# Loads of weights in an attention kernel: each quarter behind the latest transpose of probabilities, instead of four in a row

## Chip, cores and metric

The kernel runs on one core of one Trainium2 chip. The metric is the device time of one execution in microseconds; the time before is the median of three runs. Engines are named TensorE (PE in the profile, its weight loads PEld), VectorE (DVE), ScalarE (ACT), GpSimd (POOL) and SyncE (SP, which here only issues transfers).

## What is computed

Block-causal attention, then a dense mixture of four experts, then a feed-forward layer with a softmax and a layer norm in its middle:

```python
def reference(...):
    # attention: q, k, v are (4, 8, 576, 64); a query sees its block of 64 and all blocks before
    scores = scale * np.matmul(q, k.transpose(0, 1, 3, 2))
    scores = np.where(mask, scores, -1000000000.0)
    attn = np.exp(scores - np.max(scores, axis=-1, keepdims=True))
    attn = attn / (np.sum(attn, axis=-1, keepdims=True) + 1e-09)
    x = heads_to_columns(np.matmul(attn, v))          # (2304, 512)
    # mixture: w1 (4, 512, 1024), w2 (4, 1024, 512)
    for e in range(4):
        out += p[:, e:e + 1] * (np.maximum(x @ w1[e], 0.0) @ w2[e])
    # second layer: h = out @ w_in, softmax gate, layer norm, ln @ w_out
```

## The kernel before

The 2304 tokens are 18 tiles of 128 rows (`TILES`, L38): two tiles hold the first 64 rows of two batches each, called (0,0) and (2,0), and the others are tile i = 1 to 4 of batch b, called (b,i) here. They are worked through in that order. A tile (b,i) has four pairs of heads, and attention goes in steps of one pair (for i = 4, one head): TensorE makes the scores `sps`, VectorE their maximum `nm`, ScalarE the exponentials `p` (L959) and their f16 high part `hl` (L963), VectorE the low part (L964). SyncE then issues one transposing transfer per pair, `pT<-hl` (L974, in `step_b`), and TensorE multiplies pT with v into `pv` (L993). A pT of a tile with i = 1, 2, 3, 4 shows in the order as 6, 10, 14, 18 x 128. When a tile's four pairs are done, it is scaled, split in two f16 parts `xh` and transposed to `xT`, the mixture's input.

Every f32 operand of the mixture is kept as two f16 parts, so each product is three. A weight (w1 or w2 of one expert, 2 MB) goes through `w_steps` (L174): `load` takes the only buffer `stage`; four calls of `load_part` (L189) load a quarter of 512 KB each; four of `square` (L207, ScalarE) and one `scale` give the factor; four of `split` (L221) write the high part on ScalarE (L232) and the low part on VectorE (L235).

The mixture is cut in phases by expert. A phase consists of units from `phase_units` (L478): units of the first layer (`hps`, L372), whose result is evicted by ScalarE and VectorE to `hch`, and of the second (`ops`, L394). Phase 0 covers tiles 0 to 5 with expert 0, phases 1 to 3 the same tiles with the other experts, phases 4 to 7 the other twelve tiles. Phase 4 takes the weights of phase 3 once more; phase 5 loads those of expert 0 again.

The order of the work is set in two places. The loop at L1345 decides what the program emits next: an attention step, or the next entry of the list `moe` (a unit, or a piece of a weight's preparation that `spread` (L1305) has put between units). After each step it also runs up to three tasks of the list `bg`, which holds the rest of w2 of expert 0, then w1 of expert 1, then the loads and squares of w2 of expert 1:

```python
            for _ in range(3):
                if bg and bg[-1][0] <= at1.n:
                    bg.pop()[1]()
```

A scheduler then places each instruction on its engine's queue by its dependencies and by the program's order, and may put a load far ahead of the instructions that were written before it. `after` (L142) adds a dependency that costs no semaphore: it only keeps one instruction behind another in such an order. Each queue runs in order, so a transfer on SyncE's queue that waits, or is long in issue, holds up those behind it. The object `InOrder` (L81), through which all of SyncE's transfers go, is why they all show line L91.

Of the kernel before, what the change touches and what calls it, by code (L numbers as in the profile page):

```python
# [60 lines left out]
def tile_kernel(  # L61
# [17 lines left out]
    strict = [False]  # L79
# [62 lines left out]
    def after(ins, other):  # L142

        tc.add_manual_dep(
            ins.ins, other.ins.name, mybir.DependencyInfo(mybir.DependencyClass.NoSync, mybir.DependencyReason.DATA),
            reason="pace",
        )
# [11 lines left out]
    marks = {}  # L159
# [14 lines left out]
    def w_steps(key, src, bits, inv, tag, load_eng, rows=None, hi_eng=None, place_raw="stage", known=False, less=False):  # L174

        single = key in ("w_in", "w_out")
        n = F if key == "w_in" else D if key == "w_out" else src.shape[1]
        k = 4096 // n
        q = k // 4
# [9 lines left out]
        def load_part(c):  # L189
            def f():  # L190
                if single:
                    load_eng.dma_start(out=stage[key][:, c * 1024:(c + 1) * 1024], in_=src[:, c * 1024:(c + 1) * 1024])
                    return
                sv = stage[key].rearrange("p (k f) -> p k f", k=k)
                dv = src.rearrange("(k p) f -> p k f", p=128)
                m = n // 2 if less and c < 2 else n
                load_eng.dma_start(out=sv[:, c * q:(c + 1) * q, :m], in_=dv[:, c * q:(c + 1) * q, :m])
            return f

        def scale_rows(c):  # L200
# [152 lines left out]
    def flush():  # L353

        while pend:
            pend.pop(0)()
        while tail:
            tail.pop(0)()
# [382 lines left out]
    class Attention:  # L741
# [192 lines left out]
        def step_b(self, n):  # L934
            t, p, heads, last = self.steps[n]
            b, i = TILES[t]
            ps, nm = self.sPS.pop(n), self.nm_.pop(n)
            if t not in self.sums:
                self.sums[t] = sp.tile([128, NH], F32, tag="sums", name="sums")
            sums = self.sums[t]  # L940
            L = 64 + 128 * i
            W = 512 if i == 0 else 2 * L
            key = (t, p)
            if key not in self.hl_:
                self.hl_[key] = self.hlp.tile([128, 2304], F16, tag="hl", name="hl")
            hl = self.hl_[key]
            parts = [heads] if i == 0 else [(h,) for h in heads]
            for j, hh in enumerate(parts):
                pf = self.pp.tile([128, 576], F32, tag="p32", name="p32")
                n_ = W if i == 0 else L  # L950
                c0 = 0 if i == 0 else (hh[0] % 2) * L
                for x, h in enumerate(hh):
                    if i == 0:
                        src, dst = ps[:, 0, x * 128:(x + 1) * 128], pf[:, x * 128:(x + 1) * 128]
                    elif i < 4:
                        src, dst = ps[:, j, 0:L], pf[:, 0:L]
                    else:
                        src, dst = ps[:, :, 0:288], pf[:, 0:L].rearrange("p (a c) -> p a c", a=2)
                    act.activation(  # L959
                        out=dst, in_=src, func=AF.Exp, bias=nm[:, j + x:j + x + 1], scale=SCALE,  # L960
                        accum_out=sums[:, h:h + 1],
                    )
                anc["A"] = act.activation(out=hl[:, c0:c0 + n_], in_=pf[:, 0:n_], func=AF.Copy)  # L963
                anc["D"] = vec.tensor_tensor(  # L964
                    out=hl[:, W + c0:W + c0 + n_], in0=pf[:, 0:n_], in1=hl[:, c0:c0 + n_], op=ALU.subtract
                )
            if not last:
                return
            del self.hl_[key]
            if 3 <= t < FREE and n % 3 == 0:  # L970
                tt = xps[1].tile([128, 18, 128], F16, tag="xT3", name="pT")
            else:
                tt = self.tp.tile([128, 18, 128], F16, tag="pT", name="pT")
            x = sync.dma_start_transpose(out=tt[:, 0:2 * W // 128, :], in_=hl[:, 0:2 * W])  # L974
            if n < 2:
                marks["sync"] = x
            self.pT_[key] = tt

        def step_c(self, n):
# [235 lines left out]
    def load_near(odd):  # L1215
        at1.raws["near"] = near
        c = 0 if odd else S - NEAR
        src = kT[:, 0].rearrange("d (p x) s -> d p x s", x=2)[:, :, odd, c:c + NEAR]
        sync.dma_start(out=near.rearrange("d (p x) s -> d p x s", x=2)[:, :, odd], in_=src)

    def load_v(v, a, b):
        sync.dma_start(out=v, in_=vC[0, :, a:b])
        for j in range(a, b):
            at1.raws["v", 0, j] = [v[:, j - a]]
# [5 lines left out]
    def norm():  # L1230
# [9 lines left out]
        n=[lambda: load_near(0), lambda: load_near(1)], v=[lambda: load_v(vrs[0], 0, 3), lambda: load_v(vrs[1], 3, 5)], p=[load_p],  # L1240
# [64 lines left out]
    def spread(units, *spans):  # L1305

        todo = []
        for a, b, tasks in spans:
            todo += [(a + (b - a) * (k + 1) / len(tasks), fn) for k, fn in enumerate(tasks)]
        todo.sort(key=lambda x: x[0])  # L1310
        res = []
        for j, u in enumerate(units):
            while todo and todo[0][0] <= j:
                res.append((None, todo.pop(0)[1], 0.0))
            res.append(u)
        return res + [(None, fn, 0.0) for _, fn in todo]
# [9 lines left out]
    bg = [(2, fn) for fn in p1 + q1]  # L1326
    bg += [(14, fn) for fn in p2 + q2] + [(32, fn) for fn in p3]
    moe = phase_units(0, [(t, 1) for t in range(6)], psh)
    post = q3
    for j in range(1, 5):  # L1330
        us = phase_units(j, GROUPS[j // E], psh)
        n = len(us)
        if j == E - 1:
            moe += spread(us, (0, 0.1 * n, post))
            post = []
            continue
        pa, qa = next_w()
        pb, qb = next_w()
        moe += spread(us, (0, 0.1 * n, post), (0.1 * n, 0.5 * n, pa + qa), (0.5 * n, 0.9 * n, pb))
        post = qb  # L1340
    moe.reverse()
    bg.reverse()
    tpe = tdv = 0.0
    n1 = len(p2 + q2 + p3)
    while at1.more:  # L1345
        t, u, cost = moe[-1] if moe else (-1, None, 0)
        ok = t is None or t in ready and len(bg) <= n1
        if not ok or tdv <= tpe + 2.0:
            flush()
            at1.step()  # L1350
            a, c = at1.cost()
            tdv, tpe = tdv + (a * 1.2 if at1.n < SLOW else PACE + c), tpe + c
            for _ in range(3):
                if bg and bg[-1][0] <= at1.n:
                    bg.pop()[1]()
        else:
            moe.pop()
            u()
            if cost:
                flush()  # L1360
            tpe += cost
# [11 lines left out]
    n = len(moe)  # L1373
# [12 lines left out]
    for j in (5, 6, 7):  # L1386
        tasks = [[], [], [], []]
        pa, qa = next_w()
        pb, qb = next_w()
# [16 lines left out]
        post = qb  # L1406
# [174 lines left out]
```

## Time and profile before

| | |
|---|---|
| median of three runs | 1113.18 us (1112.07 to 1114.56) |
| the profiled execution | 1114.37 us, its span 1112.6 us |
| mean granted TensorE clock | 0.989 |
| busy: TensorE | 1048.0 us (94%) |
| busy: VectorE | 797.7 us (72%) |
| busy: ScalarE | 514.1 us (46%) |
| busy: GpSimd | 182.1 us (16%) |
| pT transfers | 68, median 4.3 us from issue to landing |
| loads into `stage` of 512 KB | 50, median 6.0 us from issue to landing |

Attention, with phases 0 to 3 and part of phase 4 between its steps, lies in the first 515 us or so; the rest is mixture and second layer. Shares over the whole span are averages over these parts. [...]

### The profile page before, as it was taken

Reading aid. Unit: us, or ns where it says so; the run is one execution under the profiler, and the core shown is the slowest. Engines: PE = TensorE matmul, PEld = TensorE weight load, DVE = VectorE, ACT = ScalarE, POOL = GpSimd, SP = SyncE. Lnnn points to the kernel's source line nnn. Section 1 sums busy time; section 2 is a strip of 40 time slices with the busy share of each in tenths; the row PEclk is TensorE's granted clock in tenths of the full one; section 3 lists DMA queues with packets and bytes.
Section 4 is the critical chain, followed back from the end, with each engine's and each line's share of the span. In section 5 each row is a group of like instructions: output and inputs, shape, how many; then the busy total and the mean of one; then the engine's idle time right before and its main releaser. Section 6 shows DMA issues by size and latency. Waiting matters only on the chain.

```text
span 1112.6 us, 20532 instructions
## 1 busy us (share of the span) xinstructions
PE 1048.0 (94%) x8064; PEld 657.2 (59%) x8064; DVE 797.7 (72%) x1758; ACT 514.1 (46%) x1107; POOL 182.1 (16%) x176
## 2 busy tenths in 40 slices
PE   4579889799999999999999999999999999999998
PEld 4456666465555556555576767666667674444443
DVE  7898788738768677436677656674879558999883
ACT  5667676646755455433443424232446453333222
POOL 4874633422115421000000000000000000000000
PEclk9999989799999999999999999999999999999999
DMA  9868987928877857332531212330344311434333
GB/s 303 247 164 159 249 184 163 222 79 192 193 120 178 177 147 157 64 61 48 174 114 58 77 39 76 115 133 29 95 138 128 107 27 29 95 86 88 74 85 85
DMA packets 225600, 137.95 MB, mean 124 GB/s; under 512 B 184544, under 2 KB 192736, under 8 KB 225504
## 3 DMA queue, kind: packets, MB, share of 16 engines
q1 hardware_dynamic: 225504, 136.65, 50.2%
q8 instruction: 63, 1.03, 0.4%
q14 instruction: 33, 0.27, 0.1%
HBM read 79.47 MB, written 12.06 MB: 82 GB/s over the span
## 4 chain that ended last, share of the span: by engine, by line
PE 75%; DMA 9%; DVE 7%; POOL 4%; issue 2%; ACT 2%; SPq 0%; ACTq 0%; DVEq 0%; POOLq 0%
PE ops L394 29%; PE hps L626 13%; PE hps L372 11%; PE h L1432 8%; PE o L1495 8%; DMA pT<-hl 6%; PE pv L993 3%; PE sps L912 2%; DVE hl L964 1%; PE sps L915 1%; DVE wt L235 1%; POOL wt L228 1%; DMA spill<-acc 1%; POOL ks L792 1%; POOL qlo L792 1%
## 5 line engine op out<-in xcount | busy, mean ns | idle before, releaser
L394 PE MATMUL ops<-wt,hch 128*128 128x512 f16 x1728 | 396.1, 381 | 3.7 <-DVE wt L235 1.6
L394 PEld LDWEIGHTS <-hch 128*128 128x128 f16 x1728 | 166.8, 98 | 189.9 <-issue 11.0
L372 PE MATMUL hps<-xT,wt 128*128 128x384 f16 (+1 forms) x1536 | 216.3, 291 | 2.1 <-DVE hch L383 1.3
L372 PEld LDWEIGHTS <-wt 128*128 128x128 f16 x1536 | 126.9, 100 | 62.1 <-issue 6.7
L959 ACT ACTIVATE p<-sps,nm 128x320 f32<-128x320 f32 (+4 forms) x144 | 79.0, 553 | 78.3 <-DVE nm L928 58.7
L964 DVE TENSOR_TENSOR hl<-p,hl 128x320 f16<-128x320 f32 (+4 forms) x132 | 92.3, 718 | 30.4 <-ACT hl L963 29.8
L626 PEld LDWEIGHTS <-S 128*128 128x128 f16 x1152 | 96.0, 98 | 2.8 <-issue 0.5
L1432 PE MATMUL h<-wt,x2T 128*128 128x512 f16 x432 | 95.5, 379 | 1.8 <-DVE acc L419 1.8
L1495 PE MATMUL o<-wt,lt 128*128 128x512 f16 x432 | 95.5, 379 | 0.0
L235 DVE SCALAR_TENSOR_TENSOR wt<-stage,ws,wt 128x1024 f16<-128x1024 f32 (+1 forms) x64 | 85.3, 1346 | 6.1 <-ACT wt L232 4.4
L419 DVE SCALAR_TENSOR_TENSOR acc<-ops,coef,acc 128x512 f32<-128x512 f32 x54 | 40.4, 747 | 67.2 <-PE ops L394 67.1
L912 PE MATMUL sps<-ks,qhi 128*128 128x288 f32 (+3 forms) x160 | 70.6, 443 | 18.1 <-ACT p L959 7.8
L639 ACT ACTIVATE stu<-hps 128x384 f32<-128x384 f32 x72 | 34.5, 484 | 94.7 <-PE hps L626 94.6
L626 PEld LDWEIGHTS <-wt 128*128 128x128 f16 x864 | 72.9, 98 | 6.5 <-issue 0.6
L626 PE MATMUL hps<-T,S 128*128 128x192 f16 x864 | 76.5, 246 | 0.0
L383 DVE SCALAR_TENSOR_TENSOR hch<-hps,hch 128x384 f16<-128x384 f32 (+1 forms) x98 | 53.0, 541 | 29.8 <-ACT hch L382 29.6
L1432 PEld LDWEIGHTS <-x2T 128*128 128x128 f16 x432 | 42.3, 98 | 52.9 <-issue 2.1
L993 PE MATMUL pv<-v,pT 128*128 128x64 f16 x1392 | 54.8, 196 | 19.1 <-DMA pT<-hl 19.0
L1495 PEld LDWEIGHTS <-lt 128*128 128x128 f16 x432 | 42.3, 98 | 51.0
L382 ACT ACTIVATE hch<-hps 128x384 f16<-128x384 f32 (+1 forms) x98 | 47.1, 480 | 47.7 <-PE hps L372 47.4
L232 ACT ACTIVATE wt<-stage,ws 128x1024 f16<-128x1024 f32 (+1 forms) x56 | 59.8, 1094 | 18.8 <-DVE ws L140 15.2
L993 PEld LDWEIGHTS <-pT 128*128 128x128 f16 x1392 | 50.1, 100 | 30.1 <-DMA pT<-hl 23.0
(158 smaller groups left out, 1480.6 us busy)
## 6 DMA issues: line engine op xcount, KB each, us to landing
stage<-in_w_dram SPq DMA_DIRECT2D x50, 512.0 KB, 6.0
raw<-in_qT_dram SPq DMA_DIRECT2D x34, 256.0 KB, 3.4
vraw<-in_vC_dram SPq DMA_DIRECT2D x30, 256.0 KB, 3.3
raw<-in_kT_dram SPq DMA_DIRECT2D x24, 288.0 KB, 3.6
raw<-in_w_dram SPq DMA_DIRECT2D x24, 256.0 KB, 4.0
raw<-in_w_in_dram SPq DMA_DIRECT2D x8, 512.0 KB, 4.7
raw<-in_w_out_dram SPq DMA_DIRECT2D x8, 512.0 KB, 4.3
stage<-wf SPq DMA_DIRECT2D x8, 512.0 KB, 6.1
```

What stands on the lines that cost most here:

```text
L232: h = paced_a(bg_(act.activation(out=hi, in_=r, func=AF.Copy, scale=stage[key, "s"]), "A"))
L235: stage["last"] = vec.scalar_tensor_tensor(out=lo, in0=r, scalar=stage[key, "s"], in1=hi, op0=ALU.mult, op1=ALU.subtract)
L372: pe.matmul(ps[:, j * n:j * n + n], w[:, a, kk, f * 128:(f + 1) * 128], x[:, b * KD + kk, c0:c0 + n], start=(m == 0), stop=(m == 3 * KD - 1),)
L383: marks["D"] = nc.vector.scalar_tensor_tensor(out=h[:, 1, :n], in0=ps[:, :n], scalar=0.0, in1=h[:, 0, :n], op0=ALU.max, op1=ALU.subtract)
L394: pe.matmul(ps, hch[f][:, a, o0:o0 + 128], w[:, b, f, :], start=(m == 0), stop=(m == 3 * KF - 1))
L626: i = pe.matmul(ps[x][:, jj * HT:jj * HT + HT], lhs(a, kk, jj), rhs(b, kk), start=start, stop=(m == 5), skip_group_check=not first or jj > 0,)
L912: pe.matmul(o, q, rhs, start=True, stop=False)
L959: act.activation(out=dst, in_=src, func=AF.Exp, bias=nm[:, j + x:j + x + 1], scale=SCALE, accum_out=sums[:, h:h + 1],)
L964: anc["D"] = vec.tensor_tensor(out=hl[:, W + c0:W + c0 + n_], in0=pf[:, 0:n_], in1=hl[:, c0:c0 + n_], op=ALU.subtract)
L993: pe.matmul(o, tt[:, a * nch + c, :], v[:, bb, hs], start=(m == 0), stop=(m == total - 1))
L1432: pe.matmul(ps[:, half], x[:, a * KD + kk, c:c + 128], w[:, b, kk, half * 512:half * 512 + 512], start=(m == 0), stop=(m == 3 * KD - 1),)
L1495: pe.matmul(ps, tt[:, a * KF + f], w[:, b, f], start=(m == 0), stop=(m == 3 * KF - 1))
```

## The change

Four edits: each `load_part` is kept behind the latest pT that has been emitted (`marks["pT"]`), outside the hand-written beginning; after an attention step at most one quarter is emitted from `bg`; between the units of phases 1, 2 and 4 a weight's loads are spread over a shorter stretch of their own and its squares and splits over a later one; and whatever is left in `bg` is emitted before the first unit behind phase 0.

```diff
@@ load_part
-                load_eng.dma_start(out=sv[:, c * q:(c + 1) * q, :m], in_=dv[:, c * q:(c + 1) * q, :m])
+                x = load_eng.dma_start(out=sv[:, c * q:(c + 1) * q, :m], in_=dv[:, c * q:(c + 1) * q, :m])
+                if "pT" in marks and not strict[0]:
+                    after(x, marks["pT"])
+            f.load = True
             return f
@@ step_b
             if n < 2:
                 marks["sync"] = x
+            marks["pT"] = x
             self.pT_[key] = tt
@@ the list of units
+    rest = -len(moe)
     for j in range(1, 5):
...
-        moe += spread(us, (0, 0.1 * n, post), (0.1 * n, 0.5 * n, pa + qa), (0.5 * n, 0.9 * n, pb))
+        moe += spread(
+            us, (0, 0.1 * n, post), (0.1 * n, 0.34 * n, pa[:5]), (0.34 * n, 0.54 * n, pa[5:] + qa),
+            (0.54 * n, 0.78 * n, pb[:5]), (0.78 * n, 0.95 * n, pb[5:]),
+        )
         post = qb
+    rest += len(moe)
@@ the loop
             for _ in range(3):
                 if bg and bg[-1][0] <= at1.n:
-                    bg.pop()[1]()
+                    f = bg.pop()[1]
+                    f()
+                    if hasattr(f, "load"):
+                        break
         else:
             moe.pop()
+            while bg and len(moe) < rest:
+                bg.pop()[1]()
             u()
```

What this does to the queues is seen in the order in which the built programs hold their instructions. Line numbers of the changed kernel are higher by up to 14. `stage` with 128x1024 is a quarter of a w1, with 128x2x512 of a w2.

SyncE's queue in tile (0,3), before, with w2 of expert 1:

```order
L91 DMA_TRANSPOSE pT<-hl 128x14x128
L91 DMA raw<-in_kT_dram 128x576 x2
L91 DMA_TRANSPOSE pT<-hl 128x14x128
L91 DMA stage<-in_w_dram 128x2x512 x3
L91 DMA vraw<-in_vC_dram 128x512
L91 DMA_TRANSPOSE pT<-hl 128x18x128
```

The same place in the changed kernel, with w1 of expert 1:

```order
L91 DMA_TRANSPOSE pT<-hl 128x14x128
L91 DMA stage<-in_w_dram 128x1024
L91 DMA_TRANSPOSE pT<-hl 128x14x128
L91 DMA stage<-in_w_dram 128x1024
L91 DMA_TRANSPOSE pT<-hl 128x14x128
L91 DMA stage<-in_w_dram 128x1024
L91 DMA raw<-in_qT_dram 128x512
```

The w1 stood among the pT of tile (0,1) before, two quarters and two, and moved back by two tiles; the w2 moved on to tiles (1,2) and (1,3), as one, one and two.

SyncE's queue in tile (1,3), before, with w1 of expert 2:

```order
L91 DMA_TRANSPOSE xT<-xh 128x8x128
L91 DMA_TRANSPOSE pT<-hl 128x14x128
L91 DMA raw<-in_kT_dram 128x576
L91 DMA stage<-in_w_dram 128x1024 x4
L91 DMA_TRANSPOSE pT<-hl 128x14x128
```

And in the changed kernel:

```order
L91 DMA_TRANSPOSE xT<-xh 128x8x128
L91 DMA_TRANSPOSE pT<-hl 128x14x128 x2
L91 DMA stage<-in_w_dram 128x1024 x4
L91 DMA raw<-in_kT_dram 128x576 x2
L91 DMA_TRANSPOSE pT<-hl 128x18x128
```

The four quarters still stand in a row, but behind the tile's last pT instead of ahead of it, with two loads of k and the first pT of tile (1,4) behind them.

VectorE's queue with the splits of w1 of expert 1: before, in tile (0,3) (L235 the splits, L383 evictions of the mixture's first layer):

```order
L964 TENSOR_TENSOR hl<-p_1280,hl 128x448
L235 SCALAR_TENSOR_TENSOR wt<-stage,ws,wt 128x1024
L928 TENSOR_SCALAR nm<-nm 128x1
L235 SCALAR_TENSOR_TENSOR wt<-stage,ws,wt 128x1024
L964 TENSOR_TENSOR hl<-p_1363,hl 128x448
```

In the changed kernel, in tile (0,4) (L238 the splits, L386 the evictions):

```order
L967 TENSOR_TENSOR hl<-p_1772,hl 128x576
L238 SCALAR_TENSOR_TENSOR wt<-stage,ws,wt 128x1024
L386 SCALAR_TENSOR_TENSOR hch<-hps,hch 128x384
L238 SCALAR_TENSOR_TENSOR wt<-stage,ws,wt 128x1024 x2
L386 SCALAR_TENSOR_TENSOR hch<-hps,hch 128x256
L238 SCALAR_TENSOR_TENSOR wt<-stage,ws,wt 128x1024
L930 TENSOR_REDUCE nm<-sps 128x1 x2
```

The splits moved one tile back and stand together, ahead of two maxima of scores.

## Rows read from the trace of the kernel before

**Rows 1.** The page, part 4: the chain of waits, by engine and by line.

```profile
PE 75%; DMA 9%; DVE 7%; POOL 4%; issue 2%; ACT 2%; SPq 0%; ACTq 0%; DVEq 0%; POOLq 0%
PE ops L394 29%; PE hps L626 13%; PE hps L372 11%; PE h L1432 8%; PE o L1495 8%; DMA pT<-hl 6%; PE pv L993 3%; PE sps L912 2%; DVE hl L964 1%; PE sps L915 1%; DVE wt L235 1%; POOL wt L228 1%; DMA spill<-acc 1%; POOL ks L792 1%; POOL qlo L792 1%
```

**Rows 2.** Busy time by stretch: stretch, length, PE, PEld, DVE, ACT, POOL, clock, DMA.

```profile
42.00:68.00 26.00, 17.62 (x192) 14.60 (x193) 24.21 (x49) 16.04 (x47) 25.38 (x24) 1.00 0.77 200
...
90.00:113.00 23.00, 20.91 (x271) 15.80 (x270) 21.99 (x42) 16.74 (x36) 12.98 (x11) 1.00 0.72 153
113.00:141.00 28.00, 23.38 (x347) 19.70 (x347) 19.57 (x44) 19.63 (x50) 16.76 (x16) 1.00 0.99 239
141.00:154.00 13.00, 10.24 (x109) 6.64 (x108) 12.22 (x26) 8.00 (x24) 7.18 (x8) 0.99 0.78 174
...
175.00:205.00 30.00, 23.11 (x226) 16.06 (x222) 24.96 (x44) 20.96 (x44) 15.07 (x12) 0.88 0.75 163
205.00:262.00 57.00, 57.00 (x393) 31.98 (x392) 34.50 (x65) 28.30 (x55) 12.49 (x13) 0.94 0.59 129
262.00:286.00 24.00, 21.92 (x183) 14.45 (x179) 18.23 (x40) 17.10 (x49) 7.80 (x9) 0.93 0.99 244
...
389.00:520.00 131.00, 130.44 (x1032) 76.72 (x1030) 74.92 (x168) 61.07 (x153) 13.05 (x15) 1.00 0.47 96
520.00:1113.00 593.00, 586.18 (x3982) 358.63 (x3980) 430.56 (x998) 214.62 (x374) 0.00 (x0) 1.00 0.32 88
```

**Rows 3.** Waits of TensorE, 75 to 480 us: total, times, longest.

```profile
PE pv L993 <- DMA pT<-hl: 19.0, 10, 4.3
```

**Rows 4.** Transfers issued in 191 to 195 us, with median us to landing.

```profile
stage<-in_w_dram SPq DMA_DIRECT2D x4, 512.0 KB, 7.3
...
pT<-hl SPq DMA_TRANSPOSE x1, 9.3
```

**Rows 5.** The same for 398 to 530 us.

```profile
pT<-hl SPq DMA_TRANSPOSE x14, 4.0
```

**Rows 6.** Timeline of TensorE behind that burst: start, us, what, [idle before <-releaser].

```profile
196.96 0.40 PE L912 MATMUL sps<-ks,qhi 128*128 128x288 f32 x1 [2.57 <-ACT p L959]
...
203.15 1.46 PE L993 MATMUL pv<-v,pT 128*128 128x64 f16 x24 [4.32 <-DMA pT<-hl]
```

**Rows 7.** Timeline of ScalarE at the same place.

```profile
195.04 1.06 ACT L129 ACTIVATE junk<-stage 128x1024 bf16<-128x1024 f32 x1 [2.77 <-DMA stage<-in_w_dram]
```

**Rows 8.** Busy time by windows of 10 us, columns as in rows 2.

```profile
150.00:160.00 10.00, 6.42 (x54) 5.24 (x52) 6.56 (x14) 6.71 (x20) 2.45 (x3) 0.68 0.87 219
...
190.00:200.00 10.00, 6.26 (x57) 4.19 (x55) 7.16 (x15) 4.75 (x11) 4.93 (x6) 0.90 0.97 250
200.00:210.00 10.00, 6.85 (x44) 5.10 (x45) 8.61 (x19) 8.39 (x18) 7.35 (x5) 0.50 0.88 208
210.00:220.00 10.00, 10.00 (x44) 4.32 (x43) 9.14 (x14) 5.88 (x8) 2.12 (x2) 0.92 1.11 192
270.00:280.00 10.00, 8.20 (x52) 5.20 (x53) 7.08 (x18) 7.72 (x25) 1.57 (x2) 0.83 0.85 223
```

**Rows 9.** Timeline of TensorE: other waits for pT.

```profile
121.15 1.02 PE L993 MATMUL pv<-v,pT 128*128 128x64 f16 x29 [2.24 <-DMA pT<-hl]
...
134.26 0.90 PE L993 MATMUL pv<-v,pT 128*128 128x64 f16 x25 [2.38 <-DMA pT<-hl]
...
271.80 0.52 PE L993 MATMUL pv<-v,pT 128*128 128x64 f16 x12 [2.08 <-DMA pT<-hl]
...
368.73 1.05 PE L993 MATMUL pv<-v,pT 128*128 128x64 f16 x30 [1.55 <-DMA pT<-hl]
```

**Rows 10.** Groups of VectorE, 60 to 480 us: busy us, mean ns of one.

```profile
L235 DVE SCALAR_TENSOR_TENSOR wt<-stage,ws,wt 128x1024 f16<-128x1024 f32 x29 | 41.5, 1444 | 3.5 <-ACT wt L232 2.7 <-POOL wt L228 0.8
```

**Rows 11.** Pieces of the chain of waits: start, us, what.

```profile
80.14 1.43 PE hps L372 x26
...
519.93 15.54 PE ops L394 x72
```

## The prediction

> **What bounds the kernel now.** I read the page's chain of waits first, then the busy time by stretch, then the waits inside the attention part. The chain lies 75% on TensorE and 9% on transfers, and the transfer that counts is the transpose of probabilities, pT, with 6% of the span [rows 1]. The table by stretch shows where that matters. From 520 us to the end TensorE is busy 586.2 of 593 us at full clock, so the change can win nothing there; what it can win lies in the stretches before 390 us [rows 2]. The stretch 42 to 68 is GpSimd's (25.4 of 26 us). In 90 to 113 and 141 to 154 VectorE is busy 22.0 of 23 and 12.2 of 13 us, so VectorE sets their pace. In 113 to 141, 175 to 205 and 262 to 286 no engine is full: TensorE is idle for 4.6, 6.9 and 2.1 us, and in the last two the granted clock is 0.88 and 0.93. TensorE's largest wait from 75 to 480 us is for pT, 19.0 us in 10 waits [rows 3].
>
> Why pT is late can be seen behind 191 us. SyncE issues four quarters of a weight in a row, and right behind them a pT. The quarters land after 7.3 us (median), that pT after 9.3 us [rows 4]; over 398 to 530 us, where no quarter of a weight is loaded, the median pT takes 4.0 us [rows 5]. TensorE runs dry twice, 2.57 us before scores and 4.32 us before the products with that pT [rows 6]. The 2.57 us belong to the same burst: ScalarE, which has to free the scores' buffer, sat 2.77 us in front of a square of a quarter that had not landed [rows 7]. [...]
>
> **The change, part by part.** Computation and bytes are the same; only places in the queues move.
>
> *The load of w2 for expert 1* (three quarters and one) leaves the stretch 113 to 141 for a place three tiles later, in ones and twos. TensorE waited 2.24 and 2.38 us for pT there [rows 9]: up to 4.6 us gained.
>
> *w1 for expert 1* goes the other way. Its quarters were loaded around the pT of tile (0,1), in GpSimd's stretch, and now follow the four pT of tile (0,3). So its four squares and four splits slip by about a tile, and VectorE gets the splits nearly in a row, in tile (0,4): 4 x 1.444 = 5.8 us of VectorE [rows 10] ahead of the next maxima of scores. Cost between 0 (all of it under waits for pT) and 5.8 us. I take 4.6, which cancels the gain before: the neighbouring stretches have VectorE nearly full [rows 2], so work moved among them hardly shortens them.
>
> *TensorE's filler.* In the new order fewer mixture products stand between the last pv product of tile (0,2) and that of (0,4): 192 of the first layer and 44 of the second, where there were 262 and 54. By the chain's pieces they cost 1.43/26 = 0.055 and 15.54/72 = 0.216 us each [rows 11], so 70 x 0.055 + 10 x 0.216 = 6.0 us of cover is gone there and has to be run later. Cost 0 (TensorE catches up in later gaps) to 6.0 us; I take 6.0, since the later gaps are already booked as gains below. With the thinner filler I also expect one more fall of the clock like that at 150 us, 0.32 of 10 us = 3.2 us [rows 8]; bounds 0 and the largest one seen, (0.10 + 0.50 + 0.08) x 10 = 6.8 us.
>
> *w1 for expert 2*, the burst of 191 us. In the new order it stays four in a row, but behind the last pT of tile (1,3). Between that tile's last pv products and the next tile's first stand 48 second-layer products, 48 x 0.216 = 10.4 us, longer than the 9.3 us of a delayed pT. So I take it as hidden: 2.57 + 4.32 = 6.9 us of idle time and 6.8 us of clock gained. The other end is that all of it stays.
>
> *w1 for expert 3* was four in a row ahead of a pT of tile (2,1) and is now 1, 2 and 1: the wait of 2.08 us [rows 9] and 0.17 x 10 = 1.7 us of clock [rows 8] go. *The eight loads for phase 5* stood in tile (2,4) and move to tiles (3,3) and (3,4), where TensorE is full (130.4 of 131 us from 389 to 520 [rows 2]): the wait of 1.55 us [rows 9] goes. The later squares and splits lie under the same cover.
>
> [...] The row shows what a pT pays behind four quarters, 9.3 against 4.0 us [rows 4, 5], so 5.3/4 = 1.3 us each. [...]
>
> Sum: gains 4.6 + 6.9 + 6.8 + 2.1 + 1.7 + 1.6 = 23.7 us; costs 4.6 + 6.0 + 3.2 = 13.8 us; net 9.9 us faster. The profiled execution took 1114.4 us (span 1112.6), 1.2 above the median of the runs, 1113.2. So 1114.4 - 9.9 = 1104.5 on its scale and 1103.3 as a median.
>
> **The rivals.** *The delay is spread.* Every quarter ahead of a pT costs that pT 1.3 us. Eight stand so in tiles with little cover (four of w1 in tile (0,3), four of w2 in (1,2) and (1,3)): 8 x 1.3 = 10.4 us of new waits, net 0.5 us slower, 1113.7. For it: the four-in-a-row rows scale like this. Against it: most pT waits for quiet loads never reach TensorE, since only 10 waits on pT are seen in 405 us [rows 3].
>
> *The burst of four is only moved* (the change does not do what it says, for this weight). The order still has w1 of expert 2 as four in a row, with a pT behind. If the first pT of tile (1,4) lands later than TensorE's 10.4 us of second-layer products end, the idle time and the fall of the clock come back, 6.9 + 6.8 = 13.7 us, net 3.8 us slower: 1117.0. It decides at a point that is close, 9.3 against 10.4 us. For it: two further transfers of raw k stand between burst and pT. Against it: the products wait for nothing else that is late, and tile (1,4) is the stretch with the most mixture work (205 to 262 us, where TensorE was busy all 57.0 us [rows 2]).
>
> **How the numbers follow.** Chance of the forecast 0.62, of the spread delay 0.17, of the moved burst 0.21. About 0.2%, 2.2 us, is what a measurement of this kernel can tell from no change. The forecast gives faster; of the spread delay 0.05 counts as faster (if half the quarters cost nothing, 1108.4) and 0.12 as the same; the moved burst gives slower, with 0.01 within 0.2%. Faster 0.67, same 0.13, slower 0.20. The bounds of the unknown costs: all at zero, 1113.2 - 23.7 = 1089.5; all at their upper ends (5.8 + 6.0 + 6.8) and the burst of four fully paid (13.7), 1113.2 - 23.7 + 18.6 + 13.7 = 1121.8. Eight in ten: 1091 to 1117, which takes in both rivals. The forecast's own range is 1091 to 1110.
>
> **What would show it.** Right: TensorE's waits for pT from 75 to 480 us fall from 19.0 us to about 7; the clock stays at 1.00 through the tiles (1,3), (1,4) and (2,1); TensorE's idle time appears instead in tiles (0,3) and (0,4), with VectorE's four splits in a row beside it; no pT longer than about 6 us behind a single quarter. Wrong: a pT of 9 us at the start of tile (1,4) with TensorE idle behind it and the clock at its lower level (moved burst); or many pT of 5 to 6 us with TensorE waiting 0.5 to 1.5 us for each (spread delay); or the clock falling for longer than 7 us of loss before tile (1,1) ends.

## The result, and the profile after

The changed kernel takes 1123.51 us (median of 4 runs, 1120.93 to 1124.94), the kernel before, run beside it, 1113.71 us (4 runs, 1112.07 to 1114.56). The ratio is 1.0087 with a 95% interval of [1.0063, 1.0112]: slower by 0.9%, some 9.8 us. The prediction was 1103.3 us, with a range of 1091 to 1117, and called it faster. Both are missed.

The profiled execution of the changed kernel took 1122.37 us (span 1120.4); before it was 1114.37 us (span 1112.6). First the same views as before.

The page of the changed kernel, part 4, the chain of waits by engine and by line:

```profile
PE 77%; DMA 9%; DVE 5%; issue 3%; ACT 2%; POOL 2%; SPq 1%; ACTq 0%; DVEq 0%; POOLq 0%
PE ops L397 28%; PE hps L629 14%; PE hps L375 12%; PE h L1446 8%; PE o L1509 8%; DMA pT<-hl 3%; PE pv L997 3%; DMA stage<-in_w_dram 2%; PE sps L915 1%; DVE hl L967 1%; PE sps L918 1%; DMA vraw<-in_vC_dram 1%; SPq L91 1%; DVE v L877 1%; DMA x2T<-xh 1%
```

In the chain pT's share is half of what it was (3%, 6% in [rows 1]), and the loads of weights, `stage<-in_w_dram`, stand in it with 2%.

Waits of TensorE, 75 to 480 us (total, times, longest), which answers to [rows 3]:

```profile
PE pv L997 <- DMA pT<-hl: 10.1, 9, 1.8
PE tp L219 <- DVE wt L217: 5.4, 2, 3.9
PE sps L915 <- ACT p L962: 3.9, 5, 1.5
PE pv L997 <- DVE xf L1039: 3.4, 2, 1.8
```

The change did what it was written to do. The waits for pT fell from 19.0 to 10.1 us and the longest from 4.3 to 1.8. But a new one stands behind them: `tp`, the small product that gives a weight's factor (in `scale`), with 3.9 us in one piece.

Busy time by stretch, the stretches cut near the ends of tiles, with columns as in [rows 2]:

```profile
64.00:92.00 28.00, 23.92 (x241) 15.89 (x240) 22.07 (x39) 17.43 (x52) 14.63 (x13) 0.95 0.84 188
92.00:112.00 20.00, 13.28 (x171) 11.43 (x167) 13.27 (x30) 15.92 (x37) 11.26 (x11) 0.81 0.98 232
112.00:142.00 30.00, 29.63 (x365) 23.94 (x363) 25.48 (x52) 18.15 (x40) 18.32 (x16) 0.90 0.79 179
142.00:159.00 17.00, 12.06 (x155) 9.90 (x155) 13.39 (x29) 9.79 (x31) 6.99 (x9) 0.90 0.62 150
182.00:218.00 36.00, 30.83 (x249) 18.61 (x245) 21.86 (x45) 25.50 (x52) 6.03 (x6) 0.91 0.65 176
218.00:269.00 51.00, 50.22 (x386) 29.20 (x384) 35.54 (x66) 27.45 (x56) 20.39 (x19) 1.00 0.62 146
```

The six rows are the tiles (0,2), (0,3), (0,4), (1,1), (1,3) and (1,4). In tile (0,3) TensorE is busy 13.28 of 20 us at a granted clock of 0.81 of full speed; before it was 20.91 of 23 us at 1.00 [rows 2]. As an estimate from these rows, what the clock lacks to 1.00 times the length of the stretch, the clock up to the end of (1,1) costs 0.05 x 28 + 0.19 x 20 + 0.10 x 30 + 0.10 x 17 = 9.9 us; before it was next to nothing there. Not all of that is net: in the next tile, (1,2), the kernel before loses 3.2 us to the clock [rows 8] and the changed one nothing (1.00 from 159 to 182 us). Over the whole execution the mean granted clock is 0.988, before it was 0.989; by the same estimate that is 0.012 x 1120.4 = 13.4 us against 0.011 x 1112.6 = 12.2 us: the falls moved more than they grew. Of the 7.8 us by which the span is longer, 4.0 are idle time of TensorE (68.6 us, before 64.6) and 3.8 busy time (1051.8 us, before 1048.0).

Where the time went, by the end of the last pv product of a tile (worked out from the two traces; the differences add up to the 7.8 us between the spans):

| up to the end of | before, us | after, us | added in this part |
|---|---|---|---|
| (1,1) | 154.5 | 159.3 | +4.9 |
| (1,3) | 204.6 | 218.0 | +8.5 |
| (1,4) | 262.3 | 269.0 | -6.7 |
| (2,4) | 388.9 | 394.7 | -0.9 |
| (3,4) | 514.7 | 520.5 | 0.0 |
| the end | 1112.6 | 1120.4 | +2.0 |

The 3.9 us stand in tile (1,3). Timelines of TensorE, SyncE, ScalarE and VectorE of the changed kernel there:

```profile
190.37 0.58 PE L219 MATMUL tp<-wt,ones 128*128 128x1 f32 x2 [3.90 <-DVE wt L217]
```

```profile
180.51 1.52 SPq L91 DMA_TRANSPOSE pT<-hl  x1
182.08 1.62 SPq L91 DMA_DIRECT2D stage<-in_w_dram  x2
```

```profile
186.25 1.06 ACT L129 ACTIVATE junk<-stage 128x1024 bf16<-128x1024 f32 x1 [1.76 <-DMA stage<-in_w_dram]
...
188.99 1.04 ACT L129 ACTIVATE junk<-stage 128x1024 bf16<-128x1024 f32 x1
```

```profile
190.16 0.16 DVE L217 TENSOR_REDUCE wt<-wt 128x1 f32<-128x4 f32 x1 [0.89 <-ACT junk L129]
```

Read from the bottom: TensorE waits for VectorE's sum of the four squares' results, that for ScalarE's last square at 188.99, and ScalarE had stood 1.76 us in front of the square ahead of it for a quarter that SyncE issued at 182.08, as one of the last two of w2 of expert 1. In the kernel before, with this weight in its old place, the product waited for nothing:

```profile
175.11 0.36 PE L216 MATMUL tp<-wt,ones 128*128 128x1 f32 x2
```

Behind the wait the clock falls, as windows of 10 us show beside [rows 8]:

```profile
190.00:200.00 10.00, 9.63 (x49) 5.36 (x50) 7.71 (x17) 9.32 (x19) 0.00 (x0) 0.67 0.74 145
200.00:210.00 10.00, 10.00 (x97) 6.63 (x95) 5.15 (x9) 5.11 (x12) 2.08 (x2) 1.00 0.78 258
210.00:220.00 10.00, 10.00 (x75) 5.51 (x74) 5.44 (x10) 5.66 (x12) 2.49 (x3) 1.00 0.31 76
```

The burst of four quarters of w1 of expert 2 is now issued behind 202 us, where the old one stood at 191. Transfers issued in 198 to 212 us:

```profile
stage<-in_w_dram SPq DMA_DIRECT2D x4, 512.0 KB, 5.4
...
pT<-hl SPq DMA_TRANSPOSE x1, 4.1
```

The pT in this list was issued at 198.15 us, ahead of the burst; the first one behind it follows at 217.36 us and lands after 4.6 us. The burst hurts nobody any more: TensorE is busy all 10 us of both windows from 200 us on.

### The profile page after: what moved, and what is told of

Read it like the earlier page. It is cut to its first block, busy times and chain, and to the rows that moved or that the text cites. A ratio compares the mean times of both kernels' runs of the same rounds, so it can differ in the third digit from the quotient of the medians.

```text
span 1120.4 us, 20534 instructions
## 1 busy us (share of the span) xinstructions
PE 1051.8 (94%) x8064; PEld 659.6 (59%) x8064; DVE 795.0 (71%) x1758; ACT 512.7 (46%) x1107; POOL 177.8 (16%) x176
## 4 chain that ended last, share of the span: by engine, by line
PE 77%; DMA 9%; DVE 5%; issue 3%; ACT 2%; POOL 2%; SPq 1%; ACTq 0%; DVEq 0%; POOLq 0%
PE ops L397 28%; PE hps L629 14%; PE hps L375 12%; PE h L1446 8%; PE o L1509 8%; DMA pT<-hl 3%; PE pv L997 3%; DMA stage<-in_w_dram 2%; PE sps L915 1%; DVE hl L967 1%; PE sps L918 1%; DMA vraw<-in_vC_dram 1%; SPq L91 1%; DVE v L877 1%; DMA x2T<-xh 1%
## 5 line engine op out<-in xcount | busy, mean ns | idle before, releaser
L375 PE MATMUL hps<-xT,wt 128*128 128x384 f16 (+1 forms) x1536 | 221.2, 294 | 1.9 <-ACT acc L417 1.6
L375 PEld LDWEIGHTS <-wt 128*128 128x128 f16 x1536 | 129.5, 102 | 63.1 <-issue 8.1
L967 DVE TENSOR_TENSOR hl<-p,hl 128x320 f16<-128x320 f32 (+4 forms) x132 | 86.0, 669 | 41.6 <-ACT hl L966 41.1
L238 DVE SCALAR_TENSOR_TENSOR wt<-stage,ws,wt 128x1024 f16<-128x1024 f32 (+1 forms) x64 | 87.1, 1374 | 10.0 <-ACT wt L235 6.3
L386 DVE SCALAR_TENSOR_TENSOR hch<-hps,hch 128x384 f16<-128x384 f32 (+1 forms) x98 | 52.8, 541 | 35.0 <-ACT hch L385 34.7
L629 PEld LDWEIGHTS <-wt 128*128 128x128 f16 x864 | 72.8, 98 | 5.6
L235 ACT ACTIVATE wt<-stage,ws 128x1024 f16<-128x1024 f32 (+1 forms) x56 | 59.7, 1092 | 19.1 <-DVE ws L140 14.0
L966 ACT ACTIVATE hl<-p 128x320 f16<-128x320 f32 (+4 forms) x132 | 65.2, 522 | 6.3 <-DMA pT<-hl 5.7
```

The source lines that it names most:

```text
L235: h = paced_a(bg_(act.activation(out=hi, in_=r, func=AF.Copy, scale=stage[key, "s"]), "A"))
L238: stage["last"] = vec.scalar_tensor_tensor(out=lo, in0=r, scalar=stage[key, "s"], in1=hi, op0=ALU.mult, op1=ALU.subtract)
L375: pe.matmul(ps[:, j * n:j * n + n], w[:, a, kk, f * 128:(f + 1) * 128], x[:, b * KD + kk, c0:c0 + n], start=(m == 0), stop=(m == 3 * KD - 1),)
L629: i = pe.matmul(ps[x][:, jj * HT:jj * HT + HT], lhs(a, kk, jj), rhs(b, kk), start=start, stop=(m == 5), skip_group_check=not first or jj > 0,)
L967: anc["D"] = vec.tensor_tensor(out=hl[:, W + c0:W + c0 + n_], in0=pf[:, 0:n_], in1=hl[:, c0:c0 + n_], op=ALU.subtract)
```

## The experiments

The rule `after(x, marks["pT"])` acts on each weight by itself, so it can be taken away for one. At first three theories stood: A, the loss is w1 of expert 1, moved to tile (0,3); B, it is w2 of expert 1 and the wait for its factor; C, it is in the other edits (later weights, spreading, single steps). Ratios below are to the kernel before on the same chip, whose medians were 1114.88 to 1115.65 us in these runs (1113.71 us beside the changed kernel). The ratios that tell the weights apart, in one table first:

| kernel | ratio | 95% interval |
|---|---|---|
| changed | 1.0087 | [1.0063, 1.0112] |
| before + rule on w1 of expert 1 | 1.0056 | [1.0037, 1.0074] |
| changed, w1 of expert 1 free of the rule | 0.9998 | [0.9979, 1.0017] |
| changed, w1 and w2 of expert 1 free | 0.9949 | [0.9928, 0.9970] |
| the same, run again | 0.9938 | [0.9918, 0.9959] |
| changed, no rule on any weight | 0.9974 | [0.9958, 0.9990] |
| before + rule on the later weights | 1.0112 | [1.0088, 1.0136] |

### Which weight

**The rule on w1 of expert 1 alone**, on the kernel before:

```diff
+                if "pT" in marks and not strict[0] and key == ("w1", 1):
+                    after(x, marks["pT"])
```

> The kernel before, with one edit: the quarters of w1 of expert 1, and of no other weight, are kept behind the latest pT. Theory A (this weight is the loss: its squares and splits arrive later, TensorE's filler is thin in tiles (0,3) and (0,4), and the clock falls there): 1120 to 1126 us, with some 15 to 20 us at the lower clock before tile (1,1) ends. Theory B (the loss is w2 of expert 1, whose factor TensorE now waits for in front of the product with ones): 1111 to 1116 us. Theory C (the loss is in the later weights and phases): 1111 to 1116 us.

Measured: 1121.36 us (1118.39 to 1124.94), ratio 1.0056. One load moved makes the kernel slower by 0.6%, as A has it. In its tile (0,3) TensorE is busy 12.98 of 20 us at a clock of 0.66:

```profile
91.00:111.00 20.00, 12.98 (x170) 11.32 (x167) 14.27 (x32) 18.09 (x37) 6.95 (x6) 0.66 1.15 251
```

**The changed kernel with that weight free**:

```diff
-                if "pT" in marks and not strict[0]:
+                if "pT" in marks and not strict[0] and key != ("w1", 1):
```

> The changed kernel with w1 of expert 1 alone let off the rule, so that it is loaded as early as before. Theory A: the loss of 9.8 us goes, 1108 to 1115 us. Theory B: 1119 to 1124 us, with TensorE idle for 3 to 4 us in front of the factor's product in tile (1,3) and the clock lower behind it. Theory C: 1119 to 1124 us.

Measured: 1115.89 us (1112.96 to 1119.39), ratio 0.9998. 0.89% of loss goes, so A holds for that much, but the time is no better than before, above what A asked by a little. What is left to B can be read in its trace: TensorE still waits 3.59 us at the factor of w2.

**w1 and w2 of expert 1 both free**:

```diff
-                if "pT" in marks and not strict[0]:
+                if "pT" in marks and not strict[0] and key not in (("w1", 1), ("w2", 1)):
```

> The changed kernel with w1 and w2 of expert 1 both let off the rule. Theory A: as the run that lets w1 alone off, within 3 us. Theory B: 1104 to 1113 us, some 6 us below the run that lets w1 alone off, and no idle time of TensorE over 1 us in front of a factor's product in tile (1,3). Theory C: 1119 to 1124 us.

Measured: 1110.84 us (1106.05 to 1112.85), ratio 0.9949: 0.49% less than the run before, as B has it, and below both kernels. The two factor products of w2, with w1 free and with both free:

```profile
182.17 0.38 PE L219 MATMUL tp<-wt,ones 128*128 128x1 f32 x2 [3.59 <-DVE wt L217]
```

```profile
175.12 0.28 PE L219 MATMUL tp<-wt,ones 128*128 128x1 f32 x2
```

So the rule on the two early weights costs 0.89% and 0.49%, and the rest of the change gains 0.5%. A and B both hold, C doesn't.

**No rule at all**, only spreading, single steps and the emptied list:

```diff
-                if "pT" in marks and not strict[0]:
-                    after(x, marks["pT"])
```

> The changed kernel without the rule for any weight: one quarter per step, the new spread and the emptied list stay. Theories A and B (the rule is the loss): 1106 to 1116 us. Theory C, if it is the spread of loads, squares and splits in the later phases: 1118 to 1124 us; if it is the rule on the later weights, 1106 to 1116 us, and below the run with both weights of expert 1 let off by 5 us or more.

Measured: 1112.57 us (1109.43 to 1113.91), ratio 0.9974. So half of the 0.5% comes without the rule. That the rule on the later weights brings the other half is not certain: the intervals of 0.9974 and of 0.9949 meet.

This run also tells what became of the burst of w1 of expert 2. Here its quarters stand ahead of a pT of tile (1,3), as they did before the change, and that pT is as late as in [rows 4]. SyncE's queue, the time to landing of the transfers issued in 188 to 193 us, and TensorE in front of the products with that pT:

```profile
188.87 0.81 SPq L91 DMA_DIRECT2D stage<-in_w_dram  x2
190.00 0.33 SPq L91 DMA_DIRECT2D raw<-in_qT_dram  x1
190.37 0.91 SPq L91 DMA_DIRECT2D stage<-in_w_dram  x2
192.12 4.69 SPq L91 DMA_TRANSPOSE pT<-hl  x1
```

```profile
pT<-hl SPq DMA_TRANSPOSE x1, 9.1
```

```profile
197.72 2.75 PE L395 MATMUL ops<-wt,hch 128*128 128x512 f16 x12
201.26 0.87 PE L995 MATMUL pv<-v,pT 128*128 128x64 f16 x24 [0.78 <-DMA pT<-hl]
```

TensorE waits 0.78 us where it waited 4.32 [rows 6]. The pT is no sooner, but second-layer products stand in tile (1,3), 25 by the trace, where the kernel before has none. The tiles (1,3) and (1,4) take 78.3 us, before 87.1; with the rule on all but the two early weights they take 78.1 (76.4 when run again). What they gain comes with the other edits, and hardly with the new place of the burst.

**The rule on the later weights alone**, on the kernel before:

```diff
+                if "pT" in marks and not strict[0] and key not in (("w1", 1), ("w2", 1)):
+                    after(x, marks["pT"])
```

> The kernel before with the rule for all weights but the two early ones (w1 and w2 of expert 1), and without the spreading over two stretches or the one quarter per step. If the gain of the later part (1110.84 us with both early weights freed) comes from the rule on the later weights, 1109 to 1112 us; if it comes from the spreading and the single steps, 1113 to 1116 us, with the burst of four behind 191 us still there.

Measured: 1126.68 us (1125.88 to 1130.70), ratio 1.0112. Both sides of the expectation fall: the same rule that seems to gain a little beside the other edits costs 1.1% without them. Its trace shows how. The loads are late, but the squares keep their old places in the list, so ScalarE comes to a square whose quarter has not landed, with the exponentials queued behind it, and TensorE waits for a scores' buffer. ScalarE and TensorE in tile (2,2):

```profile
288.46 1.06 ACT L129 ACTIVATE junk<-stage 128x1024 bf16<-128x1024 f32 x1 [2.60 <-DMA stage<-in_w_dram]
```

```profile
293.71 0.63 PE L915 MATMUL sps<-ks,qhi 128*128 128x320 f32 x1 [5.30 <-ACT p L962]
```

This is the stall of [rows 7] again, at twice the price for TensorE. A longer one, of 5.80 us in front of a square at 226.03 us, lies in tile (1,4), where TensorE is idle for 8.1 us and was full before. With the spreading the squares stand behind the loads by a stretch of their own. That this is what makes the rule bearable is argued; no run has the rule and the spreading without the single steps.

### What of w1 of expert 1 costs

The four loads (among the four pT of tile (0,3)) and what follows them (squares, factor, splits) moved together. These runs move them apart.

**Loads early, squares late.** From the kernel with this weight free, the squares are kept behind the latest high-part copy on ScalarE:

```diff
+                x = paced_a(bg_(squares(...), "A"))
+                if key == ("w1", 1):
+                    after(x, anc["A"])
```

> The kernel with w1 of expert 1 freed from the rule (1115.89 us), but its four squares are kept behind the latest high-part copy on ScalarE, so that squares, splits and the mixture products that need them come about as late as in the changed kernel, while the four loads stay early. Theory A1 (the cost of the rule on this weight is the traffic: four quarters among the four pT of tile (0,3)): the loads are away from there, so 1112 to 1117 us, and no fall of the clock behind tile (0,3). Theory A2 (the cost is the lateness of what follows the load: late squares and splits, and so fewer mixture products ready as TensorE's filler in tiles (0,2) to (0,4)): 1120 to 1125 us, with some 7 us of idle time in tile (0,3) and a clock of about 0.9 there.

Measured: 1124.60 us (1121.58 to 1127.47), ratio 1.0083 [1.0060, 1.0107]. With no load of a weight left in tile (0,3) all of the loss is back: A2. Its tile (0,3), 5.15 us of it idle:

```profile
90.34:109.95 19.61, 14.46 (x167) 11.60 (x167) 14.52 (x30) 15.11 (x36) 10.80 (x11) 0.75 0.86 171
```

Its queue on TensorE tells why. `tp` takes a buffer from the pool `psh` that `hps` and `ops` use too (`tp = psh.tile(..., tag="h")`). The factor of w1 of expert 1 stands behind 228 first-layer and 48 second-layer products, in this kernel, in the changed one and in the one with free loads alike. Where the squares are early it is placed in the middle of tile (0,3), and the products pass on to 292 and 66 by the tile's end. Where the squares are late it is placed behind that end, and so the count stays at 228 and 48: in the changed kernel 36 first-layer and 2 second-layer products are left in the tile to fill TensorE's waits, where there were 110 and 30. The factor is a gate for the filler. That it holds the products through the shared pool is read from the code; no run gave `tp` a buffer of its own.

**The gate moved.** The changed kernel as it is, with factor and splits of that weight written later; loads and squares keep their late places:

```diff
-    bg += [(14, fn) for fn in p2 + q2] + [(32, fn) for fn in p3]
+    bg += [(14, fn) for fn in p2[:-1]] + [(24, fn) for fn in p2[-1:] + q2] + [(32, fn) for fn in p3]
```

> The changed kernel as it is, with the rule on every weight, but the factor and the four splits of w1 of expert 1 are emitted from attention step 24 on instead of 14; its loads and squares keep their late places. The factor's product takes a buffer from the pool of the mixture's products, so mixture products emitted behind it wait for it; in the changed kernel it is late (end of tile (0,3)) and holds them at 228 first-layer and 48 second-layer ones. Here 288 and 66 stand ahead of the end of that tile. Gate theory: idle time in (0,3) falls from 6.7 us to about 2, and 1111 to 1117 us. Rival (the late loads and squares cost by themselves, by traffic or by ScalarE and VectorE work in the wrong tile): 1120 to 1125 us.

Measured: 1120.25 us, ratio 1.0045 [1.0030, 1.0059]. Idle time in (0,3) fell to 3.4 us. That is half the loss, and the median lies at the edge of what the rival said: neither theory alone.

**The gate moved and the loads early**, late squares kept; it is the kernel with loads early and squares late, with the edit of the moved gate:

```diff
+                if "pT" in marks and not strict[0] and key != ("w1", 1):
...
+                if key == ("w1", 1):
+                    after(x, anc["A"])
...
+    bg += [(14, fn) for fn in p2[:-1]] + [(24, fn) for fn in p2[-1:] + q2] + [(32, fn) for fn in p3]
```

> The kernel with late squares and early loads of w1 of expert 1 (ratio 1.0083), with its factor and splits emitted from attention step 24 on, so that the mixture products are no longer held (288 first-layer ones ahead of the end of tile (0,3)). It differs from the run with the later factor and late loads (ratio 1.0045) in the place of the four loads alone. If what is left of the cost there is the traffic of the loads among the pT of tile (0,3): about 1.000, 1112 to 1117 us. If it is the late squares and splits: about 1.0045, 1118 to 1122 us.

Measured: 1114.73 us (1113.36 to 1117.12), ratio 1.0001 [0.9988, 1.0014]. Late squares and splits cost nothing by themselves; the rest goes with the place of the loads. The four kernels that differ only in these two points, with w2 of expert 1 under the rule in all:

| ratio | factor holds the filler | factor moved |
|---|---|---|
| loads among the pT of (0,3) | 1.0087 | 1.0045 |
| loads early | 1.0083 | 1.0001 |

Either cost can be seen alone, 0.44% for the place of the loads and 0.82% for the gate, but they do not add: with the gate shut early loads gain 0.04%, where the intervals leave room for some 0.3%.

How the late loads cost is not shown. Theory A1 named the traffic among the pT. SyncE's queue with the loads late (first) and early (second):

```profile
93.18 2.07 SPq L91 DMA_TRANSPOSE pT<-hl  x1
95.30 0.79 SPq L91 DMA_DIRECT2D stage<-in_w_dram  x1
97.02 2.40 SPq L91 DMA_TRANSPOSE pT<-hl  x1
...
104.85 1.62 SPq L91 DMA_TRANSPOSE pT<-hl  x1
```

```profile
94.27 1.52 SPq L91 DMA_TRANSPOSE pT<-hl  x1
...
100.48 1.53 SPq L91 DMA_TRANSPOSE pT<-hl  x1
...
103.25 1.71 SPq L91 DMA_TRANSPOSE pT<-hl  x1
```

The pT behind the first two quarters take 2.07 and 2.40 us to issue, the one behind the third 1.62; with early loads the same three take 1.5 to 1.7. But they land after 4.4, 6.2 and 4.4 us, with early loads after 5.5, 3.9 and 4.7, and TensorE waits less for pT with the loads late. Its waits over 90 to 162 us, late and early:

```profile
PE pv L997 <- DMA pT<-hl: 4.9, 3, 2.8
```

```profile
PE pv L999 <- DMA pT<-hl: 10.3, 8, 2.2
```

So it is not by waits for pT that the late loads cost. Another way is open: ScalarE stands 1.40, 0.55 and 1.04 us in front of squares whose quarter has not landed, which does not happen with early loads, so the squares moved as well. TensorE's busy time over 90 to 162 us is the same with late and early loads, but not its clock:

```profile
90.00:162.00 72.00, 60.75 (x750) 45.67 (x748) 54.63 (x113) 45.59 (x113) 37.65 (x34) 0.93 0.81 185
```

```profile
90.00:162.00 72.00, 60.46 (x833) 47.65 (x833) 58.91 (x126) 51.12 (x132) 39.64 (x35) 1.00 0.86 183
```

With early loads TensorE gets through 833 matmuls in these 72 us, with late ones through 750. Over the whole execution, though, the clock is 0.989 with late loads and 0.990 with early ones, so a fall that is missing here stands elsewhere.

### What of w2 of expert 1 costs

**Its factor later**, from the kernel with w1 free; the product then stands behind a dozen first-layer products more:

```diff
-    bg += [(14, fn) for fn in p2 + q2] + [(32, fn) for fn in p3]
+    bg += [(14, fn) for fn in p2 + q2] + [(32, fn) for fn in p3[:-1]]
...
-    post = q3
+    post = p3[-1:] + q3
```

> The same kernel with w1 of expert 1 freed (1115.89 us), w2 of expert 1 still under the rule, but the product for its factor, in front of which TensorE stood idle 3.9 us in the changed kernel, is emitted later, behind a dozen first-layer products of phase 1. Theory B1 (what w2's late load costs is that TensorE's queue stands at this product, with the fall of the clock behind it): 1109 to 1113 us, and no wait of over 1 us in front of the factor's product. Theory B2 (the late load costs by its other effects, transfers among pT and late splits): 1114 to 1118 us.

Measured: 1116.76 us (1111.66 to 1121.42), ratio 1.0012 [0.9992, 1.0031], where 0.9998 stood: no gain, B1 falls. The wait went from the factor to a pT at the same place. SyncE and TensorE there:

```profile
176.04 1.21 SPq L91 DMA_DIRECT2D stage<-in_w_dram  x2
177.35 0.41 SPq L91 DMA_DIRECT2D raw<-in_qT_dram  x1
178.94 3.46 SPq L91 DMA_TRANSPOSE pT<-hl  x1
```

```profile
184.95 1.25 PE L997 MATMUL pv<-v,pT 128*128 128x64 f16 x20 [4.56 <-DMA pT<-hl]
```

The pT behind the last two quarters and a q takes 3.46 us to issue and lands after 6.0 us. The same pT, issued within 0.2 us of that time, lands after 5.6 us in the kernel with w1 alone free and after 4.2 us in the one with both free, which has the q there but no quarter. Two things were late at once, and the factor's wait had covered the other.

**Loaded earlier, under the rule**, from step 24 on instead of 32:

```diff
-... + [(32, fn) for fn in p3]
+... + [(24, fn) for fn in p3]
```

> The same kernel with w1 of expert 1 freed (1115.89 us); w2 of expert 1 stays under the rule but is emitted from attention step 24 on instead of 32, so that its quarters are loaded some two tiles earlier. If lateness against the factor's product is what costs, 1109 to 1113 us with no wait there; if the rule costs on any early weight, by the quarters among the pT of tile (0,4) or by the changed order of the mixture products, 1114 us or more, with idle time in tiles (0,4) and (1,1).

Measured: 1113.10 us (1111.03 to 1116.31), ratio 0.9990 [0.9972, 1.0009]. The interval takes in both no change and a small gain, and the median (1113.10) is at the edge between the two expectations; it does not settle them. Its trace shows the trade: (1,2) and (1,3) lose their wait, and (0,4) and (1,1), where the quarters now are, lose the clock:

```profile
112.00:143.00 31.00, 24.52 (x295) 19.70 (x294) 23.72 (x49) 16.26 (x42) 20.93 (x19) 0.88 0.91 202
143.00:156.00 13.00, 10.02 (x99) 8.86 (x99) 12.03 (x32) 10.83 (x31) 6.30 (x7) 0.50 1.00 268
```

**The gate of w1 moved, and w2 free**: the edit of the moved gate, and `key != ("w2", 1)` in the rule's condition.

> The kernel of the run before, with w2 of expert 1 freed from the rule as well. If the two early weights' costs add, some 0.5% below the run before: 1106 to 1112 us, no TensorE wait of over 2 us in front of a factor's product. If w2's late load costs only beside the late w1: the same as the run before.

Measured: 1113.87 us (1112.01 to 1117.88), ratio 0.9991 [0.9976, 1.0007], 0.54% below the moved gate alone (1.0045), though above the 1106 to 1112 us that were named for it. The cost of w2 adds to that of w1: 0.49% in one pair, 0.54% in the other.

**Both free, again**, beside the two with the moved gate on the same chip:

> The changed kernel with w1 and w2 of expert 1 freed from the rule, once more with five rounds, to stand beside the two runs before on the same chip: 1106 to 1113 us. If moving the factor is as good as freeing w1, within 0.3% of the run before.

Measured: 1107.69 us (1107.39 to 1111.53), ratio 0.9938 [0.9918, 0.9959]. This is the version that beats both kernels. It is 0.53% below the run before, not within 0.3%, which agrees with the 0.44% of the loads' place in the table of four. Its tiles (1,3) and (1,4):

```profile
178.00:204.00 26.00, 25.32 (x235) 15.53 (x232) 19.27 (x37) 17.65 (x36) 6.90 (x6) 1.00 0.74 152
204.00:255.00 51.00, 50.43 (x390) 29.50 (x389) 34.41 (x69) 30.52 (x63) 20.82 (x19) 1.00 0.62 160
```

## Why the prediction was wrong, step by step

Set against the runs, the prediction's sum falls into three parts, as change of time by the part of the change:

| part | booked, us | found, us |
|---|---|---|
| w2 of expert 1 | 4.6 gained | 5.5 to 6.0 lost |
| w1 of expert 1 | 13.8 lost | 9.9 lost |
| all the rest (w1 of experts 2 and 3, the loads for phase 5) | 19.1 gained | 5.7 to 6.9 gained |

What is found in the last row is the kernel with both early weights free against the kernel before (0.51 and 0.62%). Two steps failed: the gain for w2 of expert 1, off by some 10 us and with the wrong sign, and the gains for the later weights, off by 12 to 13 us. With one of them alone put right the forecast of 1103.3 us becomes some 1114 or some 1116 us; it takes both to come near the 1123.5 that were measured.

*"The load of w2 for expert 1 ... up to 4.6 us gained"* failed because it priced only the place that the load left. The two waits in tile (0,4) went (TensorE is busy 29.63 of 30 us there). At the new place the squares, the sum and the factor come behind the load, with TensorE's queue behind the factor, and the last two quarters stand ahead of a pT. Freeing this weight gains 0.49 to 0.54%. How that splits between the factor and the pT is open: moving the factor alone gained nothing, and the earlier load settled nothing.

*w1 of expert 1* was booked with 4.6 + 6.0 + 3.2 = 13.8 us; freeing it gains 0.89%, 9.9 us. The sum was high and its parts were wrong. The splits cost nothing: late squares and splits alone give 1.0001. The thin filler was the right place, and its reason, the gate in `psh`, was not named. The clock was sized at one fall of 3.2 us, bound 6.8; the rows give 9.9 us, by the estimate above, up to the end of (1,1), past the point that the prediction gave as a sign of being wrong. That loss is not added to the idle time in full, since the stretch ends only 4.9 us later.

*w1 of expert 2*, 6.9 us idle and 6.8 us of clock, 13.7 us: the waits went, but the mechanism was not the one named. The burst stands behind the tile's last pT, as predicted, and the clock is 1.00 from 200 to 220 us, where 0.50 and 0.92 stood [rows 8]. Yet without the rule, with the burst ahead of a pT that lands after 9.1 us, the waits are gone as well: the other edits put second-layer products into tile (1,3). That the term came near was luck. With both early weights free the tiles (1,3) and (1,4) take 76.4 us, from 178.2 to 254.6, where they took 87.1 before: 10.6 us gained, 3.1 of them given back in tile (1,2), which takes 23.9 us instead of 20.8. TensorE stands idle 3.19 us there for ScalarE, and ScalarE 3.58 us for a load of v; the run without any rule has the same wait (3.52 us), so it comes with the other edits. In the changed kernel the two tiles take 86.8 us: the wait for w2's factor (3.90), a pT (1.27) and the clock behind them ate the gain where it arose.

*w1 of expert 3 and the loads for phase 5*, 5.4 us: the tiles (2,1) to (2,4) gained 0.9 us. The clock stays at 1.00, and the moved loads cost nothing in (3,3) and (3,4), as said. But two pT waits of 0.88 and 1.80 us and one of 1.54 us in front of the factor of w1 of expert 3 came in place of those removed.

*Not foreseen at all*: 2.0 us behind tile (3,4), of them one wait of 1.60 us at 547 us for ScalarE's eviction into `acc`. It is there with both weights free as well (1.48 us) and without any rule (2.40 us), so it comes with the other edits; its cause was not tried.

*The rivals.* The burst was not merely moved. The spread delay has a number on its side: four quarters among the pT of tile (0,3) cost 0.44%, 4.9 us, or 1.2 us each where it had 1.3, an estimate from [rows 4, 5], though only with the gate out of the way. That agreement is luck as far as the traces go, since with the quarters there TensorE waits less for pT, 4.9 against 10.3 us, and those pT land hardly later, after 4.4, 6.2 and 4.4 us against 5.5, 3.9 and 4.7. What makes the cost is not shown by any run here.

## What to carry to other kernels

A rule that keeps a transfer at its place in the program also keeps everything behind it there: price the new place by what follows the load (here square, sum, factor, split) and by the queues on which those hold others up, not only the burst that goes away. Look for small steps that share a buffer pool with the work that fills an engine's waits; a late one holds the filler back, as the code has it here, and shows as idle time in front of quite other instructions (5.15 us in tile (0,3) with late squares). And take a rule back for one operand at a time, and then altogether: the same rule cost 1.1% alone, without two of its weights the change is worth 0.5 to 0.6%, and about half of that came without the rule, by what the other edits put under a late transfer.

## What the runs showed of the hardware

SyncE's transfers issued one after the other: in the kernel before, the pT of 193.76 us took 5.71 us to issue, and the load of k behind it began at 199.56 us. What loads cost a pT behind them went with how many stood there. Behind four quarters it landed after 9.3 us [rows 4], and after 9.1 us in the kernel without the rule; one and the same pT of tile (1,3) after 5.6 and 6.0 us behind two quarters and a q, and after 4.2 us behind the q alone; three of tile (0,3) behind single quarters after 4.4, 6.2 and 4.4 us, and after 5.5, 3.9 and 4.7 us without them. A late pT did not always cost as much: with twelve second-layer products in front (2.75 us), TensorE waited 0.78 us for the one of 9.1 us.

In windows of 1 us TensorE's granted clock was 1.00 or 0.50, and between the two only next to a window of 0.50: before, 0.50 in 20 and between in 6 of the 160 windows from 140 to 300 us; changed, 24 and 10 of the 170 from 60 to 230 us. Falls came back at places where nothing but the order had changed: 0.93 and 1.00 over the same 72 us of two kernels whose whole executions have 0.989 and 0.990, and 0.50 in tile (1,1) of the kernel with w2 loaded earlier, where the kernel before had 0.99 [rows 2]. A fall that is gone from one stretch is not yet a gain of the whole.
